# Old-state products as half tiles, and one scaled-query plane for both heads, in the first 16 units of a gated linear attention

## The chip, the cores and the metric

The kernel runs on one core of one Trainium2 chip. The metric is the device time of one execution in microseconds (us). Engines are named as the profile names them: PE (TensorE), DVE (VectorE), ACT (ScalarE), POOL (GpSimd), SP (SyncE, which here issues the DMAs).

## What is computed

A gated linear attention with 4 batches, 8 heads, 768 steps and head size 48, whose output goes through two gated layers:

```python
for t in range(S):
    state = alpha[:, :, t, :, None] * state + einsum('bhd,bhe->bhde', k[:, :, t], v[:, :, t])
    y[:, :, t] = einsum('bhd,bhde->bhe', q[:, :, t], state)
x = y.transpose(0, 2, 1, 3).reshape(B * S, H * D)
h = x @ w_in;  x = (h * cos(h)) @ w_out            # d_ff 2048
a = x @ w_a;   b = x @ w_b;  out = (a * b) @ w_out2 # d_ff 1536
```

## The kernel before

**Units.** The attention is cut into 48 units, one for each batch and each chunk of 64 steps; a unit has all 8 heads, as 4 pairs (p = 2b + c). Within a pair, head 0 lies on rows 64 to 111 and head 1 on rows 0 to 47 (`HEADS`). A unit's steps are, with the lines that the profile shows:

- DVE scans the running product of alpha (L303, tile `ar_t`), takes a reciprocal (L312), scans the other way (L315) and scales the keys (L340, tile `k`; from unit 8 on that last one is POOL's);
- POOL scales the queries into the tile `m` (L327), one operation for each head's 48 rows;
- PE makes scores (L374) and transposed keys (L383), 8 products each;
- ACT copies the keys (L389, tile `kn`), and then DVE masks the scores into `m` (L407; L413 from unit 16 on);
- PE adds up the new state (L444, and L450 for the old state) and makes the outputs: L461 is masked scores times values, and L466 the scaled queries times the old state `s`;
- ACT writes the outputs rounded to `x_t` (L505); DVE then writes the next old state `s` (L535) and the rounding rest of the outputs (L508);
- ACT sums squares for a range test (L344).

A product in f32 is two passes on PE, so 8 products are 16 passes. A unit with an old state in this form, units 1 to 11 and 13 to 15, has 8 products of L466, 224 passes in all. In units 0 to 15 (`APART`) the old state has a tile of its own; later units add it in with the values, on other code that has no L466.

**Rows of the output.** In L461, head 0 of each pair writes rows 0 to 63 of PSUM and head 1 rows 64 to 111. L466 reads 112 rows: for one head the other head's rows of `m` are zero, which is why `m` has three planes (masked scores, and scaled queries of each head beside zeros) that are cleared once at the start (L200).

**Stages.** Units 0 to 7 come first, with a small filler matmul on PE after each (L671). Then the first layer runs in six groups of 512 tokens, with 16 steps each: a projection (L656, tile `hp`), a chain of ACT and DVE operations on it (L706, L709, L714, L717, L721, L725), and the second matmul (L663). Units 8 to 15 stand between the 16 steps of the first group, units 16 to 23 between those of the second, and so on. A step of the first group also needs its weights made from 64-bit words: a DMA (L595, tile `st_t`), ACT (L599, L604), DVE (L610, L616), ACT (L625), POOL (L636). Sixteen such pairs of weights are made until the first group ends. The second layer follows.

**Order.** A planner (`Plan`) sets the order of every engine's instructions before anything runs: each operation has an engine, an assumed length in us, predecessors, and for some a due time; a list schedule over these puts the operations in a row for each engine. Operations marked `port` (two inputs in SBUF on DVE, and POOL's) are kept from overlapping in the planned time. On the chip each engine takes its row in order, so that an instruction that waits holds up all behind it.

**Lines that the change touches.** The tile `m` and its clearing (L198 to L200), the columns of a unit's input load (L284), POOL's scaled queries (L325 to L333), the scores' operand (L376), `outputs` (L455 to L471), and the assumed length of a later unit's block on PE (L494).

Of the kernel before, what the change touches and what calls it, by code (L numbers as in the profile page):

```python
# [10 lines left out]
F32 = mybir.dt.float32  # L11
# [13 lines left out]
C = 64  # L25
# [3 lines left out]
P = 128  # L29
# [28 lines left out]
NLATE = NPAIR2 - NPAIR1  # L58
DVE_DECAY = 0
# [107 lines left out]
def chunked(ctx: ExitStack, tc: tile.TileContext, u_in: bass.AP, wts: bass.AP, out: bass.AP, in_range: bass.AP):  # L167
# [30 lines left out]
    m_t = [att.tile([P, 3, NP, C], F32, name=f"m{i}", bufs=1) for i in range(3)]  # L198
    for i, t in enumerate(m_t):
        (nc.gpsimd if i else nc.vector).memset(t[:, 1:3], 0.0)  # L200
# [55 lines left out]
    def part(u, i):  # L256
        return un[u]["in"][0:112, NA + i * NC4:NA + (i + 1) * NC4].rearrange("p (c t) -> p c t", t=C)
# [16 lines left out]
    def plan_load(u):  # L274
# [3 lines left out]
        def load():  # L278
            if u < UG:
                t = wpool.tile([P, 2, 2 * DM], F32R, name="w_t").bitcast(F32)  # L280
                d["in"] = t.rearrange("p a c -> p (a c)")[:, 0:IN_COLS]
            else:
                d["in"] = att.tile([P, IN_COLS], F32, name="in_t", bufs=NIN)
            cols = W_A + 2 * NE4 if u < APART else IN_COLS  # L284
            cuts = (0, NA + 1, cols) if u == 0 else (0, cols)
            for c0, c1 in zip(cuts, cuts[1:]):
                nc.sync.dma_start(out=d["in"][:, c0:c1], in_=u_in[u, :, c0:c1])
# [5 lines left out]
    def plan_front(u):  # L293
# [20 lines left out]
        def scan_r():  # L314
# [13 lines left out]
                    m[rows, i + apart], part(u, 0)[rows], d["a"][rows, :, 1:], op=ALU.mult  # L328
# [3 lines left out]
            for rows, i in HEADS  # L332
# [29 lines left out]
    def plan_scores(u, block=None):  # L362
# [7 lines left out]
        def score():  # L370
            for c in range(2):
                for b in range(2):
                    for rows, h in HEADS:
                        nc.tensor.matmul(  # L374
                            sc_t[rows_of(b, h), b, c, :], kt[rows, 2 * b + c, :],
                            m[rows, h + apart, 2 * b + c, :], start=True, stop=True,  # L376
# [45 lines left out]
    def plan_back(u):  # L422
# [32 lines left out]
        def outputs():  # L455
            for p in range(NP):
                b, c = divmod(p, 2)
                for h, r0, n in ((0, 0, C), (1, 64, D)):
# [3 lines left out]
                        ys_t[r0:r0 + n, b, c, :], w[0:k_rows], m[0:k_rows, 0 if apart else h, p, :],  # L462
                        start=True, stop=not carry,
                    )
                    if carry:
                        nc.tensor.matmul(  # L466
                            ys_t[r0:r0 + D, b, c, :], s_t[u % 2][:, p * D:p * D + D], m[0:112, h + 1, p, :],
                            start=False, stop=True,
                        )
# [12 lines left out]
        else:  # L482
# [11 lines left out]
            us = ou = op(PE, 1.75 + (1.0 if carry else 0.0), block, [kn, ld, *mk, *ma, *before], due=due)  # L494
# [440 lines left out]
def step_by_step(  # L935
# [76 lines left out]
    with tc.For_i(0, NG, 1) as g:  # L1012
        cols = bass.ds(g * G, G)
        x = pool.tile([P, KT, G], F32, name="g_x", bufs=1)
        for j in range(KT):
            for r0, f0, n in (
                (0, 2 * j * D, D), (48, 6 * D + j, 16), (64, (2 * j + 1) * D, D), (112, 7 * D + j, 16)
# [118 lines left out]
```

## Time and profile before

| | us |
|---|---|
| median of 3 runs | 976.39 (975.45 to 978.84) |
| the profiled execution | 973.26 |
| its span in the trace | 971.4 |
| PE busy | 939.9 (97%) |
| DVE busy | 540.5 (56%) |
| ACT busy | 403.2 (42%) |
| POOL busy | 226.5 (23%) |

Busy times are unions of an engine's instructions over the whole span. They average over stages of different kinds: the first units, the first group with weights being made, the groups with units between the steps, and the second layer.

### The profile page before, as it was taken

The numbers are of one execution on the slowest core, as the hardware profiler recorded it, in microseconds if no ns is written. First come the engines' busy times: TensorE is split into PE (matmuls) and PEld (weight loads), VectorE is DVE, ScalarE is ACT, GpSimd is POOL, SyncE is SP. The second block draws the span as 40 slices with busy tenths as digits, with TensorE's granted clock in tenths as the row PEclk, the third lists the DMA queues.
The fourth block names the chain that finished last, engine by engine and source line by source line (L and its number), as shares of the span: only waits on it lengthen the run. The fifth ranks groups of instructions, "written<-read, shape, count | busy, mean of one in ns | idle before, by whom it ended". The sixth has DMA issues, their size and how long they took to land.

```text
span 971.4 us, 16849 instructions
## 1 busy us (share of the span) xinstructions
PE 939.9 (97%) x6935; PEld 766.3 (79%) x6935; DVE 540.5 (56%) x951; ACT 403.2 (42%) x754; POOL 226.5 (23%) x259
## 2 busy tenths in 40 slices
PE   6798989999999999999999999999999999999996
PEld 4677768888888888888887888888888888888884
DVE  7899998767777786776777842222222222222221
ACT  3477755545545455446665523112113113112111
POOL 4556543313322232312224321001001001000000
PEclk8999999999999999999999999999999999999998
DMA  9355412212221221203223400000000000000000
GB/s 369 106 199 184 164 38 78 90 62 81 88 63 54 89 89 54 64 1 139 98 98 112 149 0 33 1 1 33 1 0 33 1 1 33 0 1 33 1 1 36
DMA packets 17700, 64.96 MB, mean 67 GB/s; under 512 B 2384, under 2 KB 4816, under 8 KB 17616
## 3 DMA queue, kind: packets, MB, share of 16 engines
q1 hardware_dynamic: 17616, 63.81, 19.0%
q8 instruction: 56, 0.92, 0.4%
q14 instruction: 28, 0.23, 0.1%
HBM read 56.72 MB, written 4.72 MB: 63 GB/s over the span
## 4 chain that ended last, share of the span: by engine, by line
PE 87%; DVE 6%; DMA 2%; ACT 2%; issue 1%; POOL 1%; SPq 0%; ACTq 0%
PE acc_t L663 33%; PE hp L656 18%; PE xy L656 15%; PE ap L656 15%; PE xy L461 2%; DMA st_t<-wts 2%; PE xy L374 1%; DVE wf_t L610 1%; DVE wf_t L616 1%; DMA w_t<-u_in 1%; PE xy L383 1%; DVE c_t L709 1%; DVE ar_t L303 1%; PE xy L444 1%; DVE glo_t L725 1%
## 5 line engine op out<-in xcount | busy, mean ns | idle before, releaser
L663 PE MATMUL acc_t<-ghi_t,w_t 128*128 128x512 f32 x972 | 301.1, 391 | 1.0 <-ACT ghi_t L721 1.0
L656 PE MATMUL hp<-x_t,w_t 128*128 128x512 f32 (+1 forms) x882 | 216.4, 390 | 3.2 <-DMA x_t<-x_t 3.2
L663 PEld LDWEIGHTS acc_t<-ghi_t,w_t 128*128 128x128 f32 x972 | 181.6, 188 | 39.3 <-ACT ghi_t L721 1.9
L663 PE MATMUL acc_t<-glo_t,w_t 128*128 128x512 f32 x486 | 190.1, 391 | 3.8 <-DVE glo_t L725 3.8
L822 DVE TENSOR_TENSOR xy<-c_t,xy 128x512 f32<-128x512 f32 x72 | 50.1, 696 | 258.0 <-PE xy L656 257.9
L656 PEld LDWEIGHTS hp<-x_t,w_t 128*128 128x128 f32 x882 | 161.1, 188 | 36.8 <-ACT w_t L625 3.3
L656 PE MATMUL xy<-x_t,w_t 128*128 128x512 f32 x594 | 145.6, 390 | 0.0
L656 PE MATMUL ap<-x_t,w_t 128*128 128x512 f32 x540 | 132.2, 389 | 0.0
L656 PEld LDWEIGHTS xy<-x_t,w_t 128*128 128x128 f32 x594 | 111.5, 188 | 23.4
L656 PEld LDWEIGHTS ap<-x_t,w_t 128*128 128x128 f32 x540 | 101.4, 188 | 21.1
L819 ACT COPY c_t<-ap 128x512 f32<-128x512 f32 x72 | 42.3, 587 | 167.9 <-PE ap L656 167.8
L663 PEld LDWEIGHTS acc_t<-glo_t,w_t 128*128 128x128 f32 x486 | 91.2, 188 | 25.6 <-DVE glo_t L725 6.4
L826 ACT CAST ghi_t<-xy 128x512 fp32r<-128x512 f32 x72 | 42.2, 586 | 138.3 <-DVE xy L822 138.3
L706 ACT ACTIVATE c_t<-hp 128x512 int32<-128x512 f32 x96 | 57.5, 599 | 67.4 <-PE hp L656 67.1
L636 POOL TENSOR_TENSOR w_t<-wf_t,w_t 128x768 fp32r<-128x768 f32 x32 | 64.0, 1999 | 92.1 <-ACT w_t L625 92.1
L781 POOL TENSOR_TENSOR x_t<-x,x_t 128x512 fp32r<-128x512 f32 x18 | 23.7, 1343 | 251.0 <-ACT x_t L778 251.0
L714 ACT ACTIVATE c_t<-c_t 128x512 f32<-128x512 f32 x96 | 60.6, 631 | 46.7 <-DVE c_t L709 45.9
L709 DVE CUSTOM_DVE_ANT_0 c_t<-c_t,hp 128x512 f32<-128x512 int32 x96 | 65.6, 683 | 25.6 <-ACT c_t L706 24.7
L721 ACT CAST ghi_t<-hp 128x512 fp32r<-128x512 f32 x96 | 56.4, 587 | 54.1 <-DVE hp L717 53.5
L717 DVE TENSOR_TENSOR hp<-c_t,hp 128x512 f32<-128x512 f32 x96 | 65.8, 685 | 19.7 <-ACT c_t L714 19.2
L830 DVE TENSOR_TENSOR glo_t<-xy,ghi_t 128x512 fp32r<-128x512 f32 x72 | 49.8, 692 | 47.3 <-ACT ghi_t L826 47.3
L725 DVE TENSOR_TENSOR glo_t<-hp,ghi_t 128x512 fp32r<-128x512 f32 x96 | 65.7, 684 | 17.1 <-ACT ghi_t L721 16.3
(100 smaller groups left out, 923.3 us busy)
## 6 DMA issues: line engine op xcount, KB each, us to landing
st_t<-wts SPq DMA_DIRECT2D x34, 768.0 KB, 4.3
in_t<-u_in SPq DMA_DIRECT2D x32, 626.0 KB, 3.8
in_t<-u_in SPq DMA_DIRECT2D x8, 578.0 KB, 9.5
out<-o_t SPq DMA_DIRECT2D x18, 256.0 KB, 2.1
w_t<-u_in SPq DMA_DIRECT2D x7, 578.0 KB, 7.8
x_t<-x_t SPq DMA_DIRECT2D x48, 48.0 KB, 2.9
w_t<-u_in SPq DMA_DIRECT2D x1, 447.5 KB, 3.5
w_t<-u_in SPq DMA_DIRECT2D x1, 130.5 KB, 2.2
```

The costliest lines, as they stand in the source:

```text
L636: nc.gpsimd.tensor_tensor(t[:, 1], conv.pop(i), t[:, 0].bitcast(F32), op=ALU.subtract)
L656: nc.tensor.matmul(acc, wt[:, w, j * P:(j + 1) * P], r[:, j, :], start=i == 0, stop=i == len(terms) - 1)
L663: nc.tensor.matmul(accs[j], wt[:, w, j * P:(j + 1) * P], r, start=first and i == 0, stop=last and i == 2)
L706: nc.scalar.activation(s["c"].bitcast(I32), s["u"], AF.Identity, bias=-0.25, scale=-1.0)
L709: nc.vector._custom_dve(TENSOR_ADD_SAT, out=s["c"], in0=s["c"].bitcast(I32), in1=s["u"], s0=0.25, s1=-0.75)
L714: nc.scalar.activation(s["c"], s["c"], AF.Sin, bias=math.pi / 2, scale=TWO_PI)
L717: nc.vector.tensor_tensor(s["u"], s["c"], s["u"], op=ALU.mult)
L721: nc.scalar.copy(s["hi"], s["u"])
L725: nc.vector.tensor_tensor(s["lo"], s["u"], s["hi"].bitcast(F32), op=ALU.subtract)
L819: nc.scalar.copy(s["c"], s["a"])
L822: nc.vector.tensor_tensor(s["b"], s["c"], s["b"], op=ALU.mult)
L830: nc.vector.tensor_tensor(s["lo"], s["b"], s["hi"].bitcast(F32), op=ALU.subtract)
```

## The change

In units 0 to 15 the scaled queries of both heads go into one plane of `m` by one POOL operation over 112 rows, in place of two operations over 48 rows into two planes; the tile has two planes, and it is no longer cleared at the start. A product with the old state then reads only its own head's 48 rows, of `s` and of `m`, and stands after the 8 products of L461 in place of between them, in the order that L374 has: c, b, head. The heads write the rows of the output that `rows_of(b, h)` names, so that in pairs 2 and 3 head 0 is on rows 64 to 111; the host's order of the first weights and the fallback follow that. A load of units 0 to 15 has 16 more columns. The planner is told that a later unit's block takes 1.5 us on PE in place of 1.75, plus 0.85 in place of 1.0 where there is an old state.

```diff
-    m_t = [att.tile([P, 3, NP, C], F32, name=f"m{i}", bufs=1) for i in range(3)]
-    for i, t in enumerate(m_t):
-        (nc.gpsimd if i else nc.vector).memset(t[:, 1:3], 0.0)
+    m_t = [att.tile([P, 2, NP, C], F32, name=f"m{i}", bufs=1) for i in range(3)]
...
-            cols = W_A + 2 * NE4 if u < APART else IN_COLS
+            cols = W_A + 2 * NE4 + C - D if u < APART else IN_COLS
...
-                    m[rows, i + apart], part(u, 0)[rows], d["a"][rows, :, 1:], op=ALU.mult
+                    m[rows, i], part(u, 0)[rows], d["a"][rows, :, 1:], op=ALU.mult
...
-            for rows, i in HEADS
+            for rows, i in (((slice(0, 112), 1),) if apart else HEADS)
...
-                            m[rows, h + apart, 2 * b + c, :], start=True, stop=True,
+                            m[rows, 1 if apart else h, 2 * b + c, :], start=True, stop=True,
...
-                for h, r0, n in ((0, 0, C), (1, 64, D)):
+                for h in range(2):
+                    rows = rows_of(b, h)
+                    n = D if rows.start else C
                     w = d["in"][:, W_A + h * NE4 + p * D:W_A + h * NE4 + p * D + n]
                     k_rows = P if apart or h else 112
                     nc.tensor.matmul(
-                        ys_t[r0:r0 + n, b, c, :], w[0:k_rows], m[0:k_rows, 0 if apart else h, p, :],
-                        start=True, stop=not carry,
+                        ys_t[rows.start:rows.start + n, b, c, :], w[0:k_rows], m[0:k_rows, 0 if apart else h, p, :],
+                        start=not carry or c == 0, stop=not carry,
                     )
-                    if carry:
-                        nc.tensor.matmul(
-                            ys_t[r0:r0 + D, b, c, :], s_t[u % 2][:, p * D:p * D + D], m[0:112, h + 1, p, :],
-                            start=False, stop=True,
-                        )
+            if carry:
+                for c in range(2):
+                    for b in range(2):
+                        for rows, h in HEADS:
+                            p, r0 = 2 * b + c, rows_of(b, h).start
+                            nc.tensor.matmul(
+                                ys_t[r0:r0 + D, b, c, :], s_t[u % 2][rows, p * D:p * D + D], m[rows, 1, p, :],
+                                start=False, stop=c == 1,
+                            )
...
-            us = ou = op(PE, 1.75 + (1.0 if carry else 0.0), block, [kn, ld, *mk, *ma, *before], due=due)
+            us = ou = op(PE, 1.5 + (0.85 if carry else 0.0), block, [kn, ld, *mk, *ma, *before], due=due)
```

With other lengths and one POOL operation fewer, the planner puts the instructions of all engines in another order. Line numbers shift too: up to one less before the outputs, five more after them.

ACT near the start, before: `kn0` and `kn1` are the copied keys of even and odd units, `x_t` the outputs (of unit 0, on `xy`, then of unit 1, on `acc_t`), and `wf_t` the first pair of weights.

```order
L505 ACTIVATE x_t_210<-xy_119 112x4x64
L344 ACTIVATE w_t_142,ranges_113<-ar_t_156 112x520
L389 COPY kn1_110<-acc_t_120 128x4x48
L344 ACTIVATE w_t_144,ranges_113<-ar_t_182 112x520
L599 ACTIVATE wf_t_279<-st_t_216 128x768
L505 ACTIVATE x_t_210<-acc_t_120 112x4x64
L389 COPY kn0_109<-xy_119 128x4x48
```

The same place now, from the square sum of unit 2 on:

```order
L343 ACTIVATE w_t_141,ranges_110<-ar_t_199 112x520
L510 ACTIVATE x_t_220<-acc_t_117 112x4x64
L388 COPY kn0_106<-xy_116 128x4x48
L604 ACTIVATE wf_t_317<-st_t_255 128x768
L343 ACTIVATE w_t_147,ranges_110<-ar_t_260 112x520
L388 COPY kn1_107<-acc_t_117 128x4x48
L510 ACTIVATE x_t_220<-xy_116 112x4x64
```

The first weights' conversion stood ahead of the outputs of unit 1; now it stands behind them and behind the keys of unit 2, and ahead of the keys of unit 3 and the outputs of unit 2.

DVE near the start, before, from the reciprocal of unit 1 on (scans are printed as SCALAR_TENSOR_TENSOR with `first` or `last`): `m0` and `m1` are the masked scores of units 0 and 1, `k1` and `k0` the keys of units 1 and 2, `s1` the old state for unit 1.

```order
L312 RECIPROCAL last_91<-ar_t_156 112x4
L315 SCALAR_TENSOR_TENSOR ar_t_156<-w_t_142,last_91 112x260
L340 TENSOR_TENSOR k1_108<-ar_t_156,w_t_142 112x256
L303 SCALAR_TENSOR_TENSOR ar_t_182<-w_t_144,first_90 112x260
L407 TENSOR_TENSOR m0_99<-xy_119,mask_95 128x256
L312 RECIPROCAL last_91<-ar_t_182 112x4
L315 SCALAR_TENSOR_TENSOR ar_t_182<-w_t_144,last_91 112x260
L340 TENSOR_TENSOR k0_107<-ar_t_182,w_t_144 112x256
L303 SCALAR_TENSOR_TENSOR ar_t_212<-w_t_150,first_90 112x260
L535 TENSOR_TENSOR s1_106<-xy_119,ar_t_146 112x192
L508 SCALAR_TENSOR_TENSOR x_t_210<-xy_119,x_t_210 112x4x64
```

The same place now:

```order
L311 RECIPROCAL last_91<-ar_t_153 112x4
L314 SCALAR_TENSOR_TENSOR ar_t_153<-w_t_139,last_91 112x260
L406 TENSOR_TENSOR m0_99<-xy_116,mask_95 128x256
L339 TENSOR_TENSOR k1_105<-ar_t_153,w_t_139 112x256
L302 SCALAR_TENSOR_TENSOR ar_t_199<-w_t_141,first_90 112x260
L311 RECIPROCAL last_91<-ar_t_199 112x4
L540 TENSOR_TENSOR s1_103<-xy_116,ar_t_143 112x192
L406 TENSOR_TENSOR m1_100<-acc_t_117,mask_95 128x256
L314 SCALAR_TENSOR_TENSOR ar_t_199<-w_t_141,last_91 112x260
L339 TENSOR_TENSOR k0_104<-ar_t_199,w_t_141 112x256
L513 SCALAR_TENSOR_TENSOR x_t_220<-xy_116,x_t_220 112x4x64
```

The mask of unit 0 moved ahead of the keys of unit 1 and of the first scan of unit 2, and the next state and the mask of unit 1 ahead of the second scan of unit 2; scans of units further on moved behind.

DVE at the fourth pair of weights, before (`wf_t` with two numbers is that pair and the next; `ar_t` with `first` is the scan of a unit further on):

```order
L709 ISA c_t_796<-c_t_796,hp_756 128x512
L616 SCALAR_TENSOR_TENSOR wf_t_754<-st_t_545,wf_t_754 128x768
L717 TENSOR_TENSOR hp_756<-c_t_796,hp_756 128x512
L303 SCALAR_TENSOR_TENSOR ar_t_855<-in_t_389,first_90 112x260
L610 SCALAR_TENSOR_TENSOR wf_t_848<-wf_t_848,st_t_680 128x768
L535 TENSOR_TENSOR s0_105<-xy_119,ar_t_643 112x192
L312 RECIPROCAL last_91<-ar_t_855 112x4
L725 TENSOR_TENSOR glo_t_877<-hp_756,ghi_t_872 128x512
```

The same place now:

```order
L714 ISA c_t_779<-c_t_779,hp_741 128x512
L621 SCALAR_TENSOR_TENSOR wf_t_739<-st_t_610,wf_t_739 128x768
L722 TENSOR_TENSOR hp_741<-c_t_779,hp_741 128x512
L615 SCALAR_TENSOR_TENSOR wf_t_766<-wf_t_766,st_t_655 128x768
L302 SCALAR_TENSOR_TENSOR ar_t_855<-in_t_410,first_90 112x260
L730 TENSOR_TENSOR glo_t_860<-hp_741,ghi_t_853 128x512
L540 TENSOR_TENSOR s0_102<-xy_116,ar_t_638 112x192
L714 ISA c_t_845<-c_t_845,hp_789 128x512
```

The first conversion of the next pair stood behind the scan; now it stands ahead of it.

## Rows read from the trace of the kernel before

**Rows 1.** A row for each stretch; the first line names the columns
```profile
core 0: us, PE busy (x) PEld busy (x) DVE busy (x) ACT busy (x) POOL busy (x), PEclk, DMA share, GB/s
0.00:41.00 41.00, 30.91 (x684) 23.20 (x684) 30.14 (x67) 17.90 (x41) 19.12 (x33) 0.92 0.67 257
41.00:134.00 93.00, 81.27 (x914) 65.06 (x914) 87.93 (x128) 65.86 (x119) 56.34 (x42) 0.98 0.48 162
134.00:437.00 303.00, 303.00 (x3034) 245.55 (x3034) 229.73 (x493) 153.09 (x319) 91.24 (x149) 1.00 0.20 65
```

**Rows 2.** Timeline of ACT, then DVE: start us, us, instruction, [idle before <- releaser]
```profile
18.62 0.90 ACT L599 ACTIVATE wf_t<-st_t 128x768 f32<-128x768 f32 x1 [5.53 <-DMA st_t<-wts]
19.43 0.36 ACT L505 ACTIVATE x_t<-acc_t 112x256 fp32r<-112x256 f32 x1
19.70 0.30 ACT L389 COPY kn<-xy 128x192 f32<-128x192 f32 x1
...
20.69 0.63 ACT L344 ACTIVATE w_t<-ar_t 112x520 f32<-112x520 f32 x1
21.21 0.20 ACT L344 ACTIVATION_READ_ACCUMULATOR w_t<-ar_t 112x1 f32 x1
...
19.41 0.43 DVE L340 TENSOR_TENSOR k<-ar_t,w_t 112x256 f32<-112x256 f32 x1 [3.16 <-PE xy L383]
...
20.10 0.41 DVE L407 TENSOR_TENSOR m<-xy,mask 128x256 f32<-128x256 f32 x1
```

**Rows 3.** The chain that ended last, first units: start us, us, what
```profile
32.46 0.56 PE acc_t L450 x4
33.03 0.26 PE acc_t L461 x3
...
34.13 0.19 PE acc_t L671
...
41.21 0.39 ACT x_t L505
```

**Rows 4.** Timeline around the first projection step, DVE and PE
```profile
41.63 0.43 DVE L508 SCALAR_TENSOR_TENSOR x_t<-acc_t,x_t 112x256 fp32r<-112x256 f32 x1 [0.41 <-ACT x_t L505]
41.97 0.35 DVE L535 TENSOR_TENSOR s<-acc_t,ar_t 112x192 f32<-112x192 f32 x1
...
43.05 0.93 DVE L616 SCALAR_TENSOR_TENSOR wf_t<-st_t,wf_t 128x768 int32<-128x768 int32 x1
...
45.72 1.44 PE L656 MATMUL hp<-x_t,w_t 128*128 128x256 f32 x9 [3.22 <-DMA x_t<-x_t]
```

**Rows 5.** The chain that ended last, unit 9 on PE
```profile
57.02 0.33 PE xy L461 x4
57.34 0.12 PE xy L466 x4
...
58.16 0.39 PE xy L374 x16
58.55 0.22 PE xy L383 x16
```

**Rows 6.** Groups by line from 41 to 134 us: xcount, busy us, mean ns
```profile
L610 DVE SCALAR_TENSOR_TENSOR wf_t<-wf_t,st_t 128x768 int32<-128x768 int32 x15 | 20.9, 1396 | 0.1
L616 DVE SCALAR_TENSOR_TENSOR wf_t<-st_t,wf_t 128x768 int32<-128x768 int32 x15 | 17.2, 1150 | 0.0
L303 DVE TENSOR_TENSOR_SCAN ar_t<-in_t,first 112x260 f32<-112x260 f32 x8 | 11.0, 1380 | 0.0
...
L636 POOL TENSOR_TENSOR w_t<-wf_t,w_t 128x768 fp32r<-128x768 f32 x15 | 29.7, 1981 | 24.1 <-ACT w_t L625 24.1
L327 POOL TENSOR_TENSOR m<-in_t,ar_t 48x256 f32<-48x256 f32 x18 | 17.6, 977 | 4.7 <-DVE ar_t L303 4.0
```

**Rows 7.** One line, whole execution: xcount, ns min/median/max, first and last start
```profile
L610 DVE SCALAR_TENSOR_TENSOR wf_t<-wf_t,st_t x34: 923/954/3280, 32.2 to 562.1; 128x768 int32<-128x768 int32 x34
...
L303 DVE TENSOR_TENSOR_SCAN ar_t<-in_t,first x40: 666/700/2998, 35.4 to 409.6; 112x260 f32<-112x260 f32 x40
```

More of the change, by code (lines that the diff above doesn't have):

```diff
@@ L58 @@
 NLATE = NPAIR2 - NPAIR1
+LOW, HIGH = (0, 2, 5, 7), (1, 3, 4, 6)
 DVE_DECAY = 0
@@ L1016, in step_by_step @@
             for r0, f0, n in (
-                (0, 2 * j * D, D), (48, 6 * D + j, 16), (64, (2 * j + 1) * D, D), (112, 7 * D + j, 16)
+                (0, LOW[j] * D, D), (48, LOW[3] * D + j, 16), (64, HIGH[j] * D, D), (112, HIGH[3] * D + j, 16)
             ):
@@ L1107 @@
     perm = np.stack([
-        np.concatenate([rows[2 * j], rows[6, j::KT], rows[2 * j + 1], rows[7, j::KT]])
+        np.concatenate([rows[LOW[j]], rows[LOW[3], j::KT], rows[HIGH[j]], rows[HIGH[3], j::KT]])
         for j in range(KT)
```

## The prediction

> **What bounds the kernel now.** I first cut the execution into stretches [rows 1]. From 134 us on PE is busy without a gap (303.00 of 303.00 us): from there the end is PE's remaining work, and nothing that ACT, DVE or POOL gain there counts. From 41 to 134 us, where the weights of the first group are made, DVE is busy 87.93 of 93 us, PE 81.27 and POOL 56.34. In the first 41 us no engine is full: PE 30.9, DVE 30.1, POOL 19.1. So the first 134 us are what can shrink, and a saving on PE alone is worth little in them.
>
> Next I read what the first units wait for. ACT takes its row in order, and from 13.1 to 18.62 us it stands 5.53 us before the first weights' conversion L599, until its DMA lands [rows 2]. Behind that stood the outputs of unit 1 (L505, at 19.43, 0.81 us after the conversion began). DVE waited 3.16 us meanwhile. From there on the units follow one another: the outputs of unit 7 are read at 41.21 [rows 3], so six units took 21.78 us, 3.63 each. Then the first projection's second half waits on PE for the DMA of the outputs of units 4 to 7, until 45.72 [rows 4], 3.66 us after DVE finished them (41.63 + 0.43).
>
> In the stretch from 41 to 134 us DVE's own rows are longer than they need be. L610 takes 1396 ns there on average and L303 1380 ns [rows 6], where their medians are 954 and 700 ns, and single ones take up to 3280 and 2998 ns [rows 7]. Over the counts that is 15 x 0.44 = 6.6 us, 8 x 0.68 = 5.4 us, and for L616, which has L610's shape, 15 x 0.20 = 2.9 us: 14.9 us in all. These operations read two inputs in SBUF, as POOL's do; L717 and its like, which read PSUM, are not among the long ones. I take the long ones for waits for a POOL operation that has begun, mostly the weights' L636 of 1.98 us [rows 6]. I call one a lock.
>
> **The order at the start: -3.4 us.** This is the largest term, and it comes from the planner's new order, not from the work removed. ACT's row now has the outputs of unit 1 and the keys of unit 2 ahead of the first conversion. I assume that the DMA lands when it did; each input load grows by 16 columns on 1156, 1.4%, which I cost at nothing (at most 1.4% of the 18.62 us until then, 0.3 us). When the wait ends at 18.62, one unit more is done. Then ACT has the conversion (0.8 us until the next one starts), a square sum with its read-out (20.69 to 21.41, 0.72 us) and the keys of unit 3 (0.30 us) [rows 2]: keys of unit 3 ready at 20.5.
>
> From keys to keys a unit now goes through: mask 0.41 [rows 2], new keys' product on half tiles 0.22 [rows 5], old state 0.56 [rows 3], L461 0.26 [rows 3] and three further groups of 0.12 [rows 5], together 0.62, the half tiles of the old-state products 0.39 (below), the filler matmul 0.19 [rows 3], scores and transposes 0.39 + 0.22 [rows 5], keys' copy 0.30: 3.30 us. For four changes of engine I add 0.2 (one is 0.03: 41.60 to 41.63 [rows 3, 4]): 3.5 us. Keys of unit 7 come at 20.5 + 4 x 3.5 = 34.5, and its outputs are read 0.41 + 0.22 + 0.56 + 0.62 + 0.39 = 2.2 us and a change or two later, at 36.9 in place of 41.21: 4.3 us sooner. At the old pace of 3.63 it would be 3.8.
>
> How much of this survives? On PE, the second half of the first projection: outputs done at 36.9 + 0.39 + 0.43 = 37.7, plus the DMA's 3.66, gives 41.4 in place of 45.72: -4.3. On DVE, the end of the second pair's L616: from 37.3, what its new row has up to there, 0.43 + 0.35 [rows 4], two scans of 0.70 and an L610 and an L616 of 0.95 [rows 7], ends at 41.4 in place of 43.98 [rows 4]: -2.6. The next stage hangs on DVE more than on PE, and on both; I take the middle, -3.4, with -2.6 and -4.3 as ends.
>
> **POOL's one operation for two: -0.5 us.** Sixteen of 32 operations go. In units 8 to 15 that is 8 of the 18 L327 of the stretch, at 0.98 us [rows 6], 7.8 of POOL's 56.34 us. POOL isn't full there, and waits 24.1 us for ACT before L636 alone. If locks fell with POOL's time, it would be 14.9 x 7.8 / 56.34 = 2.1 us; if all are L636's, nothing. I take 0.5, nearer to nothing, since a single L303 of 3.0 us holds more than an L327. For units 0 to 7 the saving is within the pace above, in which POOL's row doesn't come last.
>
> **The old-state products on PE: 0.** In unit 9 they are half of 32 passes from 57.02 to 58.16, 1.14 us, in groups of four of 0.12 us, so two passes run side by side [rows 5]. Scores and transposes are half tiles of the shape that L466 gets: 16 passes in 0.39 us behind products of full rows, and in 0.22 without such a change [rows 5], so four run side by side and the change of shape costs 0.17. For units 8 to 11 and 13 to 15, where scores follow, it is now 0.33 + 3 x 0.12 + 0.39 + 0.22 = 1.30 us to the end of the scores in place of 1.53 (57.02 to 58.55): 7 x 0.23 = 1.6 us less. PE idles 11.7 us in that stretch [rows 1], so I credit nothing; the end is 1.6 if PE is what waits last. In units 1 to 7 the sum is 1.01 in place of 1.10 (33.03 to 34.13 [rows 3]), which is in the pace, and the filler behind it changes shape once more, beside ACT.
>
> Here a page speaks against the change. In L374 and L383 the two heads of a pair stand on different row halves and write one PSUM bank, and the 16 passes still take 0.22 us, a quarter of what they would take one by one. The Trainium skill, TensorEngine Tiling (Array Packing), section Restrictions and Gotchas, says under Gotcha 1 that different row tiles can't access the same PSUM bank at one time; by that they would go in pairs at best, 0.46 us, and the row disagrees.
>
> **Edits at nothing.** The cleared planes (three operations) ran before the first input was there. From unit 16 on, head 1 follows head 1 on the same rows once in each output block. The halves go in pairs now, and I expect each half to keep its own row; if not, a pass of 0.06 us [rows 5] is added in each of 32 blocks, in a stretch that PE bounds: +1.8 at most. The planner's 1.5 for 1.75 us moves steps of later groups by a place; PE has no gap there for it to cost or win.
>
> **The sum.** -3.4 - 0.5 = -3.9 us. The profiled execution took 973.26 us (span 971.4), 3.1 below the median of the runs, and would take 969.4; on the median's footing 976.39 - 3.9 = 972.5.
>
> **The rivals.**
> Slower: more locks. The new order puts L610 ahead of the scan at the fourth pair of weights, right where POOL's L636 of the third or fourth starts, and other places change likewise. Each lock costs DVE up to 1.98 us. There are now 14.9 us of them, worth about eight. Two more undo the gain, three and a half make it a loss beyond 0.3%; four more give -3.9 + 7.9 = +4.0, 980.4 us. For it: fifteen L636 meet some forty two-input operations, with nothing on the chip that keeps them apart. Against it: the patterns behind each L616 look alike in both orders.
>
> Little change: the lead is spent. The first conversion on DVE stands behind the units' work as before, so the first pair and the projections come no sooner, and DVE in the next stage is 95% busy. If a third of DVE's smaller lead lasts, -2.6 / 3 = -0.9: 975.5.
>
> Much faster: three locks fewer, -5.9, with the lead of 3.4: -9.3, 967.1. PE's idle 11.7 us would allow it.
>
> The half tiles don't run four abreast: 0.46 for 0.22 in the five units from 3 to 7, +1.2, so -2.7: 973.7. The page above has this; the rows of L374 speak against it.
>
> **How the numbers follow.** A measurement of this kernel can tell about 0.3% (2.9 us) from no change, so faster means under 973.5. The forecast has 0.46; its own ends are -4.3 - 2.1 - 1.6 = -8.0 and -2.6 + 1.8 = -0.8, and four fifths of it lie under 973.5. More locks 0.12, the lead spent 0.26, fewer locks 0.13, paired half tiles 0.03. Faster: 0.37 + 0.13 + 0.02 = 0.52; same: 0.09 + 0.26 + 0.01 = 0.36; slower: 0.12. The range goes from 967.0, with fewer locks just inside, to 978.5, where half of the slower case is out.
>
> **What would show it.** In the changed kernel ACT's wait for the first weights should end near 18.6 us with the outputs of unit 1 already done, the outputs of unit 7 be read near 37 us, and the first projection's second half start near 41.5. L466's passes should come in groups of four of some 0.06 us. L610, L616 and L303 should have the same 14 to 15 us above their medians, less half a microsecond. PE should run without a gap from about 130 us on. It is wrong if the conversion's DMA lands later, if L610 and L303 in that stretch lengthen, or if PE waits as long as before for the first group's weights.

## The result: slower, and the clock of the first units is why

| | median of the runs, us | profiled execution, us | span, us | mean granted clock |
|---|---|---|---|---|
| before | 975.92 (975.3 to 978.84) | 973.26 | 971.4 | 0.991 |
| after | 986.18 (984.71 to 989.16) | 985.47 | 983.7 | 0.966 |

The ratio is 1.0103 with a 95% interval of 1.0071 to 1.0135: the changed kernel is slower by some 10 us, where 972.5 was forecast, and outside the range of 967.0 to 978.5. Here and below, a median is of all executions of a kernel but those over 1,050 us (four in all, two of them of the kernel before). A ratio is to the executions of before that were taken beside it, and leaves out those that lie over 1.5% above the fastest of their kernel, among them some with a low clock.

The page of after shows where to look before any wait is read. Its forty slices of the span give PE's busy share and the clock that it was granted, in tenths:

```profile
PE   7779989999999999999999999999999999999996
...
PEclk7559999999999999999999999999999999999998
```

The second and third slice, some 25 to 74 us, stand at half. The same in ten-microsecond stretches of after (busy time of each engine, then PEclk, DMA share, GB/s):

```profile
core 0: us, PE busy (x) PEld busy (x) DVE busy (x) ACT busy (x) POOL busy (x), PEclk, DMA share, GB/s
10.00:20.00 10.00, 8.16 (x158) 6.41 (x154) 4.95 (x13) 3.88 (x11) 1.36 (x2) 0.57 1.02 417
20.00:30.00 10.00, 7.70 (x144) 5.68 (x140) 4.72 (x12) 3.94 (x9) 1.36 (x2) 0.50 0.60 238
30.00:40.00 10.00, 8.29 (x138) 6.60 (x138) 5.19 (x13) 3.42 (x8) 1.37 (x2) 0.50 0.08 22
40.00:50.00 10.00, 7.52 (x139) 5.67 (x136) 4.74 (x10) 2.18 (x7) 0.00 (x0) 0.50 0.01 2
50.00:60.00 10.00, 7.71 (x67) 6.36 (x70) 7.00 (x12) 3.94 (x6) 5.40 (x5) 0.50 0.37 113
60.00:70.00 10.00, 7.19 (x130) 6.82 (x123) 6.14 (x11) 6.04 (x13) 4.81 (x4) 0.53 0.56 205
70.00:80.00 10.00, 10.00 (x121) 8.11 (x120) 8.20 (x15) 7.09 (x14) 3.87 (x4) 1.00 0.43 140
```

TensorE runs at 1.2 GHz (granted 0.50) from 11.5 to 69.5 us, 58 us long. In the kernel before it did so from 12.6 to 19.4 and from 46.7 to 50.1, 10.2 us together. Two stretches of the kernel before:

```profile
20.00:30.00 10.00, 7.75 (x221) 6.49 (x223) 7.76 (x20) 7.12 (x16) 2.71 (x4) 1.00 0.59 234
30.00:40.00 10.00, 8.99 (x247) 7.44 (x243) 7.68 (x17) 5.04 (x11) 4.92 (x6) 1.00 0.31 102
```

A busy PE hides this: 7.5 busy microseconds of ten look like a PE that works as it did, but at half the clock. DVE, whose mask takes 0.42 us here and took 0.41 before [rows 2], shows it: from 20 to 40 us it is busy 4.72 and 5.19 of ten, for 7.76 and 7.68.

Against [rows 1], the first three stretches of after:

```profile
0.00:41.00 41.00, 31.69 (x521) 22.71 (x525) 20.88 (x51) 14.64 (x33) 7.40 (x19) 0.64 0.62 240
41.00:134.00 93.00, 83.90 (x1054) 68.20 (x1047) 75.99 (x125) 65.17 (x119) 49.71 (x33) 0.85 0.48 165
134.00:437.00 303.00, 300.33 (x2958) 242.76 (x2957) 232.41 (x493) 153.28 (x320) 95.70 (x151) 0.99 0.21 67
```

PE is as busy in the first 41 us (31.69 for 30.91), and does 521 matmuls in them where it did 684. This is one unit of after on PE (start us, us, instruction, idle time before it and who ended it):

```profile
17.79 0.68 PE L443 MATMUL xy<-w_t,kn 64*48 64x48 f32 x16 [0.94 <-DVE m L406]
18.39 1.06 PE L449 MATMUL xy<-s,ident 112*112 112x96 f32 x4
19.38 1.12 PE L462 MATMUL xy<-m,w_t 128*64 128x64 f32 x16
20.43 0.68 PE L471 MATMUL xy<-m,s 48*48 48x64 f32 x16
21.04 0.63 PE L676 MATMUL acc_t<-zeros 128*64 128x512 bf16 x1
22.28 0.70 PE L373 MATMUL acc_t<-m,k 48*64 48x64 f32 x16 [0.61 <-DVE x_t L513]
```

PE works 4 to 5 us and then waits 0.94 us for the mask; that wait stands ahead of every unit's new keys. A unit takes some 6 us here. The 0.61 us before L373 come from the filler: the operation of DVE that L373 waits for waited in its turn for L676, which writes a bank of the tile that it reads,

```profile
21.71 0.42 DVE L513 SCALAR_TENSOR_TENSOR x_t<-acc_t,x_t 112x256 fp32r<-112x256 f32 x1 [2.92 <-PE acc_t L676]
```

and this comes back in every second unit (at 22.28, 34.67 and 47.07).

What ACT and PE say of the forecast's own places (rows of after that answer to [rows 2, 3, 4]):

```profile
15.84 0.38 ACT L510 ACTIVATE x_t<-acc_t 112x256 fp32r<-112x256 f32 x1 [2.10 <-PE acc_t L676]
...
18.09 0.90 ACT L604 ACTIVATE wf_t<-st_t 128x768 f32<-128x768 f32 x1 [0.82 <-DMA st_t<-wts]
...
53.03 0.38 ACT L510 ACTIVATE x_t<-acc_t 112x256 fp32r<-112x256 f32 x1 [2.25 <-PE acc_t L676]
...
57.50 2.26 PE L661 MATMUL hp<-x_t,w_t 128*128 128x256 f32 x9 [2.29 <-DMA x_t<-x_t]
```

ACT's long wait went as forecast: 0.82 us for 5.53 [rows 2], with the outputs of unit 1 read before it. But the outputs of unit 7 are read at 53.03, against 41.21 [rows 3], and the projection's second half begins at 57.50, against 45.72 [rows 4]: 11.8 us later at both places. The span ends 12.3 us later.

### The profile page after: what moved, and what is told of

Read it like the earlier page. It is cut to its first block, busy times and chain, and to the rows that moved or that the text cites. A ratio compares the mean times of both kernels' runs of the same rounds, so it can differ in the third digit from the quotient of the medians.

```text
span 983.7 us, 16811 instructions
## 1 busy us (share of the span) xinstructions
PE 953.4 (97%) x6935; PEld 776.4 (79%) x6935; DVE 530.1 (54%) x950; ACT 404.9 (41%) x754; POOL 213.6 (22%) x241
## 3 DMA queue, kind: packets, MB, share of 16 engines
HBM read 56.85 MB, written 4.72 MB: 63 GB/s over the span
## 4 chain that ended last, share of the span: by engine, by line
PE 91%; DVE 4%; DMA 2%; ACT 1%; issue 1%; SPq 0%; ACTq 0%; DVEq 0%
PE acc_t L668 33%; PE hp L661 19%; PE xy L661 15%; PE ap L661 15%; PE xy L462 3%; DMA st_t<-wts 2%; PE xy L373 2%; PE xy L443 1%; PE xy L382 1%; DVE wf_t L621 1%; PE xy L449 1%; DMA w_t<-u_in 1%; DVE wf_t L615 0%; PE acc_t L676 0%; PE acc_t L462 0%
## 5 line engine op out<-in xcount | busy, mean ns | idle before, releaser
L661 PE MATMUL hp<-x_t,w_t 128*128 128x512 f32 (+1 forms) x882 | 219.4, 395 | 2.3 <-DMA x_t<-x_t 2.3
L661 PEld LDWEIGHTS hp<-x_t,w_t 128*128 128x128 f32 x882 | 164.0, 193 | 36.9 <-issue 3.0
L827 DVE TENSOR_TENSOR xy<-c_t,xy 128x512 f32<-128x512 f32 x72 | 50.1, 696 | 258.0 <-PE xy L661 257.9
L722 DVE TENSOR_TENSOR hp<-c_t,hp 128x512 f32<-128x512 f32 x96 | 65.7, 684 | 20.1 <-ACT c_t L719 20.1
L726 ACT CAST ghi_t<-hp 128x512 fp32r<-128x512 f32 x96 | 56.4, 587 | 48.2 <-DVE hp L722 47.7
```

The lines of the kernel that those rows point to most:

```text
L661: nc.tensor.matmul(acc, wt[:, w, j * P:(j + 1) * P], r[:, j, :], start=i == 0, stop=i == len(terms) - 1)
L722: nc.vector.tensor_tensor(s["u"], s["c"], s["u"], op=ALU.mult)
L726: nc.scalar.copy(s["hi"], s["u"])
L827: nc.vector.tensor_tensor(s["b"], s["c"], s["b"], op=ALU.mult)
```

## The experiments

Each execution comes with its mean granted clock. That turned out to be what tells one execution of a kernel from another, so I count an execution as **clock up** from 0.984 on; the profiled one of before, with 10.2 us at 1.2 GHz in its first 70, has 0.991, that of after 0.966. The border is mine, set after the clocks were known, and no gap in the numbers marks it: those of before run from 0.979 to 0.992. Where the executions of a kernel lie far apart, the median and the count of clock up say more than the ratio.

| kernel | median, us | ratio to before [95%] | clock up |
|---|---|---|---|
| before | 975.8 | | 90 of 120 |
| after | 986.2 | 1.0103 [1.0071, 1.0135] | 0 of 4 |
| half tiles, old order | 979.2 | 1.0026 [1.0014, 1.0038] | 0 of 10 |
| old instructions, new order | 980.8 | 1.0034 [1.0007, 1.0061] | 4 of 10 |
| after, products over 112 rows | 985.0 | 1.0098 [1.0079, 1.0116] | 0 of 6 |
| after, two POOL operations | 989.0 | 1.0138 [1.0109, 1.0167] | 0 of 6 |
| after, 2 fillers a unit | 981.9 | 1.0057 [1.0035, 1.0078] | 0 of 10 |
| after, 3 more in the gap | 979.0 | 1.0040 [1.0013, 1.0067] | 7 of 12 |
| before, 3 more in the gap | 979.6 | 1.0053 [1.0036, 1.0070] | 5 of 5 |
| half tiles, old order, 3 more | 982.2 | 1.0058 [1.0027, 1.0089] | 5 of 12 |
| after, filler in a free bank | 982.2 | 1.0087 [1.0053, 1.0121] | 1 of 6 |
| after, free bank, 2 more | 971.7 | 0.9978 [0.9957, 0.9999] | 11 of 12 |
| after, free bank, 4 more | 972.8 | 0.9965 [0.9944, 0.9986] | 11 of 11 |
| before, free bank, 4 more | 978.2 | 1.0023 [1.0005, 1.0042] | 12 of 12 |
| half tiles, old order, free bank, 4 more | 974.2 | 0.9982 [0.9968, 0.9996] | 12 of 12 |
| after, free bank, 4 more in units 0 to 2 | 978.3 | 0.9996 [0.9971, 1.0021] | 3 of 12 |
| after, free bank, 4 more from unit 3 | 972.9 | 0.9987 [0.9965, 1.0009] | 9 of 12 |
| before without filler | 976.4 | 1.0002 [0.9981, 1.0022] | 6 of 12 |

### One part of the change at a time

**Half tiles in the old order.** The changed instructions in the order of the kernel before, held there by an empty second POOL step in the plan and the old lengths:

```diff
+            ma = [
+                op(POOL, 0.7, lambda: scale_q(slice(0, 112), 1), [sa, *m_before], port=True),
+                op(POOL, 0.7, lambda: None, [sa, *m_before], port=True),
+            ]
-            us = ou = op(PE, 1.5 + (0.85 if carry else 0.0), block, [kn, ld, *mk, *ma, *before], due=due)
+            us = ou = op(PE, 1.75 + (1.0 if carry else 0.0), block, [kn, ld, *mk, *ma, *before], due=due)
```

> The changed kernel's instructions (half tiles, one POOL operation for the scaled queries) in the order of the kernel before: the planner is given the old lengths and an empty second POOL operation. Theory FORM (half tiles keep PE at the half clock through the first units, whatever the order): the clock falls near 12 us and stays at 1.2 GHz until about 70 us, time 984 to 988 us. Theory ORDER (the new order spaces PE's work so that the clock doesn't rise again): the clock is back by about 20 us as before, time 973 to 977 us.

979.2 us; in the profiled execution 1.2 GHz from 11.2 to 48.8.

**The old instructions in the new order.** Both POOL operations in one planned step, and the new lengths:

```diff
+        def both():
+            for rows, i in HEADS:
+                scale_q(rows, i)
+            ma = [op(POOL, 0.7, both, [sa, *m_before], port=True)]
-            us = ou = op(PE, 1.75 + (1.0 if carry else 0.0), block, [kn, ld, *mk, *ma, *before], due=due)
+            us = ou = op(PE, 1.5 + (0.85 if carry else 0.0), block, [kn, ld, *mk, *ma, *before], due=due)
```

> The kernel before's instructions (old-state products on 112 rows, two POOL operations, cleared planes) in the order of the changed kernel. Theory FORM: the clock rises again by about 20 us, and the lead of the new order, 3 to 4 us, shows: 970 to 974 us. Theory ORDER: the clock stays at 1.2 GHz until about 70 us as in the changed kernel, 985 to 989 us.

980.8 us, but the executions range from 973.0 at a clock of 0.990 to 988.8 at 0.969: one program, 16 us apart, and the clock goes with it. So neither theory stands alone: each half of the change costs 3 to 5 us and both together 10.

**Products over 112 rows.** If half tiles were what kept the clock down, full rows in the changed kernel would bring it back:

```diff
-    ys_t[r0:r0 + D, b, c, :], s_t[u % 2][rows, p * D:p * D + D], m[rows, 1, p, :],
+    ys_t[r0:r0 + D, b, c, :], s_t[u % 2][0:112, p * D:p * D + D], m[0:112, 1, p, :],
```

> The changed kernel with each old-state product over 112 rows of both operands instead of one head's 48, so that no two of them run side by side by rows; its place in the order, POOL's one operation and everything else stay. Its sums take in the other head, so the outputs differ; the work it times is that of full tiles. Theory FORM (PE's shorter burst per unit with half tiles is what keeps the clock down): the clock rises before 30 us and the time is 976 to 981, as for the old instructions in the new order (980.8). Rival ORDER (the spacing alone keeps it down): 1.2 GHz to past 45 us, 984 to 987.

985.0: in the new order the rows of the tiles are not what costs the time. The clock of the profiled execution did rise before 30 us, as FORM had it, but only from 22.2 to 25.6; it was at 1.2 GHz again until 46.1. The run also bounds what half tiles cost or gain as such where the clock is down: 986.2 against 985.0, with intervals that overlap. In the old order half tiles were not taken apart from POOL's one operation.

**Two POOL operations into the one plane**, rows 64 to 111 and 0 to 63:

```diff
+        def both():
+            for rows in (slice(64, 112), slice(0, 64)):
+                scale_q(rows, 1)
```

> The changed kernel with its scaled queries made by two operations on POOL, one head's rows each, into the same plane; order and half tiles as changed. Theory GAP (POOL's operation ends before PE asks for it either way, so the gap for the mask stays 0.93 us): within 1.5 us of the changed kernel, 984 to 988. Rival POOL (the single operation shifts the units' spacing so that the clock stays down): 979 to 982, as for the old instructions in the new order.

989.0, with 2.8 us more than after and intervals that still overlap: POOL's one operation doesn't cause the loss, and may be worth a gain. What else sets the old instructions in the new order (980.8) apart from these two, such as the alternation of L461 and L466, was not tried.

### Filler

**More filler behind the outputs, and none.** Two matmuls of zeros in place of one behind each unit of after; and the kernel before with none there (`keep_warm(0)`).

```diff
-                keep_warm(1)
+                keep_warm(2)
```

> The changed kernel with two filler matmuls in place of one after each of the first eight units, nothing else. If the half clock is what costs the time, and more PE work holds it up, the clock is back at 2.4 GHz by about 20 us and the time is 970 to 975 us, 11 to 16 us below the changed kernel; FORM and ORDER both allow it. If the time comes from something else (POOL and DVE in each other's way, weights that come late), it stays within 1 us of 986, or gets worse by 8 fillers of 0.2 to 0.6 us, 2 to 5 us.

981.9, 4 us less than after; 1.2 GHz from 22.2 to 53.0 us and from 56.4 to 66.6 in the profiled execution, in place of 11.5 to 69.5. The rise by 20 us and the 970 to 975 us didn't come: this filler is too little, or stands in the wrong place.

> The kernel before without the filler matmul after each of the first eight units. If the clock in the first units hangs on how much PE has to do, it should stay at 1.2 GHz here too, until 60 to 70 us, and the time be 983 to 990 us with the old form and the old order. If the old form or the old order alone is enough to bring the clock back, it is at 2.4 GHz from about 20 us and the time is 974 to 977 us.

A single execution took 973.3 us, at a clock of 0.989; twelve more show no gain:

> The kernel before without the filler behind the outputs of units 0 to 7 (15 at the start stay), which took 973.3 in one run. If that holds, its filler costs 2 us and the clock needs no filler in the old form: 972.5 to 974.5. Rival (chance in the single run): 975 to 977.

976.4, with 6 of 12 executions clock up, where 90 of 120 are with the filler. That is too few to show that the filler is worth something to the clock in the old form; on the time the two agree.

**Three more where PE waits for the mask**, behind the transposes of units 0 to 8, in three kernels:

```diff
+            def front():
+                for fn in ops["emit"]:
+                    fn()
+                keep_warm(3)
```

> The changed kernel with three further filler matmuls behind the transposes of units 0 to 8, where PE waits 0.90 to 0.94 us for the mask; no other instruction moves. Theory CLOCK (all that was lost is lost because PE stays at 1.2 GHz through the first units; the change's own work would gain what was forecast): the granted clock is at 2.4 GHz from about 25 us at the latest, the three fillers (0.64 us at 2.4 GHz) lie inside the wait, and the time is 971 to 974. Rival LATER (the order of DVE and POOL in the weights' stretch loses as well): the clock rises as early, the time stays at 977 or more. Rival SPACING (filler cannot hold the clock up in this order): 1.2 GHz until past 45 us again, 980 or more.

> The kernel before with the same three fillers behind the transposes of units 0 to 8: the control for the run above. Theory CLOCK: the kernel before has only 10 us at 1.2 GHz in its first 70 us, so filler can give it at most half of that on PE and nothing where ACT's wait sets the pace: 975 to 976.5. Rival (filler is worth several us in any form, so that the run above says nothing on the change): 972 or less.

> Half tiles and POOL's one operation in the order of the kernel before, with the same three fillers: clock held up, the old order. It prices the new order with the clock equal. Forecast's first term (the new order is worth 3.4 us where the clock is up): 975 to 976, 3 to 4 us above the changed kernel with the same fillers. Rival (the lead is spent in the weights' stretch): within 1 us of it. Rival LATER: 2 us or more below it.

The executions of after fall in two: seven at 976.0 to 979.3 with a clock of 0.986 and more, five at 989.3 to 995.3 with 0.973 and less. So the clock went as CLOCK had it in seven and as SPACING had it in five, and CLOCK's time, 971 to 974, came in none: filler cost the kernel before 3.8 us, too. The trace of after with three fillers, an execution with a low clock, shows one way in which it costs (ACT's read of a unit's outputs):

```profile
16.13 0.38 ACT L515 ACTIVATE x_t<-acc_t 112x256 fp32r<-112x256 f32 x1 [1.91 <-PE acc_t L681]
```

L681 is the filler. It writes the accumulator's first bank and the odd units stand in the other two of the same tile, so ACT waits for filler that was issued behind the outputs. (It is not the only way: four fillers in a bank of their own, below, still cost the kernel before 2.3 us.) Where the clock was up, half tiles in the old order took 976.3 and in the new order 978.0, before 979.6: the first sign that half tiles and POOL gain and that the order doesn't.

**The filler in a bank that no unit uses**, four in the gap:

```diff
-        warm = acc_t[:, 0]
+        warm = bank("hp", "hp", 3)
...
+                keep_warm(4)
```

> The changed kernel with four filler matmuls behind the transposes of units 0 to 8, and with all filler written to a bank that no unit uses, so that no reader of a unit's bank waits for a filler (in the run with three fillers ACT's read of the outputs waited 1.91 us for them). Theory CLOCK: the clock stays at 2.4 GHz from 20 us on at the latest and the time is 971 to 975; with the clock equal, the runs with three fillers put the new order 1.6 us above the old one and half tiles with POOL's one operation some 3 us below full tiles, so 973 to 974 here. Forecast's first term (the order gains 3.4 us where the clock is up): 970 to 972, and 3 us below the same kernel in the old order. Rival SPACING (filler in the gaps does not hold the clock up): 1.2 GHz past 45 us in most runs, 980 or more.

> The kernel before with the same four fillers in the free bank. Theory CLOCK with filler off the path: 974 to 976, as the kernel before, since its clock is up anyway. Rival (the fillers themselves cost, as the three in a unit's bank did: 980.4): 979 or more.

> Half tiles and POOL's one operation in the old order, with the same four fillers in the free bank. Theory CLOCK, from the runs with three fillers (976.3 where the clock was up, against 979.5 for full tiles): 971 to 973, the fastest of the three. Forecast's first term: 975 to 976, 3 us above the new order. Rival (half tiles keep the clock down whatever fills the gaps): 980 or more with 1.2 GHz past 40 us.

The clock is up in all 35 executions counted. The changed kernel takes 972.8, 3.0 us less than the kernel before; with the same filler it is 5.3 us below the old form. Its first units, the same stretches and columns as above:

```profile
10.00:20.00 10.00, 9.94 (x229) 6.50 (x225) 6.29 (x16) 4.26 (x13) 2.05 (x3) 1.00 1.02 418
20.00:30.00 10.00, 9.16 (x208) 6.30 (x210) 7.86 (x20) 6.35 (x15) 1.37 (x2) 1.00 0.70 269
```

229 matmuls, the fillers among them, in the ten microseconds from 10 on, for 158 of after.

**The bank alone, and two fillers.**

> The changed kernel with its filler written to a bank that no unit uses, no filler added. Theory GAP (the clock stays down since PE has a gap of 0.93 us in every unit): 1.2 GHz to past 45 us as in the changed kernel, 984 to 987. Rival BANK (what the four-filler run gained came from readers that no longer wait for a filler): 973 to 977.

> The changed kernel with two fillers in the gap in place of four, in the free bank. Theory GAP: two fill 0.43 of the 0.93 us at 2.4 GHz and 0.86 at 1.2 GHz; the clock is up in most runs but falls in some, 973 to 979, with a wider spread than with four (973.0). Rival BANK: as with the bank alone, within 1 us.

The bank alone leaves 982.2 in the middle, and gives what I could not have ordered: its profiled execution kept the clock (0.988) and took 972.48, the other five 980.6 to 988.7 at 0.964 to 0.974. Order and work are those of after; only the place that filler is written to differs. That place may have a part in the time as well: the five at a low clock have a median of 983.6, 2.6 us under after, with ranges that overlap. The clock of the one execution stays up until 43.3, and is at 1.2 GHz from there to 57.0:

```profile
10.00:20.00 10.00, 6.96 (x213) 5.29 (x208) 6.16 (x17) 4.20 (x13) 2.05 (x3) 1.00 1.02 419
```

though PE waits for the mask in every unit as before, 0.94 us; this is one unit of it on PE:

```profile
15.86 0.45 PE L443 MATMUL xy<-w_t,kn 64*48 64x48 f32 x16 [0.94 <-DVE m L406]
16.24 0.63 PE L449 MATMUL xy<-s,ident 112*112 112x96 f32 x4
16.80 0.68 PE L462 MATMUL xy<-m,w_t 128*64 128x64 f32 x16
17.41 0.44 PE L471 MATMUL xy<-m,s 48*48 48x64 f32 x16
17.78 0.40 PE L676 MATMUL hp<-zeros 128*64 128x512 bf16 x1
18.12 0.46 PE L373 MATMUL acc_t<-m,k 48*64 48x64 f32 x16
```

Beside the unit of after above, these rows are the cost of the clock: L449 0.63 for 1.06, L462 0.68 for 1.12, L471 0.44 for 0.68. With two fillers the clock is up in 11 of 12 executions and the median is 971.7, the lowest of all.

**Early gaps or late ones.** The four fillers in the gaps of units 0 to 2 alone, and (with `u >= 3`) in those of units 3 to 8 alone:

```diff
-                keep_warm(4)
+                keep_warm(4 if u < 3 else 0)
```

> The changed kernel, filler in the free bank, four more behind the transposes of units 0 to 2 alone. Theory START (a clock that is up at the third unit stays up, gaps of 0.94 us or not, as in the one fast run with the bank alone): 971 to 974 in nearly all runs. Rival GAPS (the gaps of the later units pull it down again): falls to 1.2 GHz between 20 and 35 us in most runs, 976 to 984.

> The same, with the four fillers behind the transposes of units 3 to 8 alone. Theory START: the clock falls near 11.5 us in most runs as in the changed kernel, and comes back only when units 3 and 4 leave PE no gap at 1.2 GHz (1.7 us of filler in 0.93): up from 30 us at the latest, 974 to 977. Rival GAPS: what the later gaps pull down doesn't come, 971 to 974, as with filler in all units.

Filler in units 0 to 2 alone leaves the clock up in 3 of 12 (978.3; 1.2 GHz from 20.1 to 64.5 in the profiled one), filler from unit 3 on in 9 of 12 (972.9). START fell: with the first three gaps filled the clock stayed up in only 3 of 12. The gaps of the later units count, and filling them suffices in most executions.

## Why the prediction was wrong, point by point

**The step that failed: every duration of PE was taken at 2.4 GHz.** The term "order at the start" sums a unit to 3.5 us from rows of the kernel before whose matmuls ran at the full clock, and carries that clock over to an order in which it didn't hold. The PEclk of 0.92 stands in [rows 1], and the working never asks what kept it there. At 1.2 GHz a unit takes 6 us, seven of them come 11.8 us late, and the rest of the kernel, which PE bounds, starts that much later.

The execution with the bank alone, against after, shows what the clock did (ACT and PE, columns as above):

```profile
38.02 0.38 ACT L510 ACTIVATE x_t<-acc_t 112x256 fp32r<-112x256 f32 x1 [0.38 <-PE acc_t L471]
...
42.48 1.59 PE L661 MATMUL hp<-x_t,w_t 128*128 128x256 f32 x9 [1.91 <-DMA x_t<-x_t]
```

Outputs of unit 7 at 38.02 for 53.03, the second half at 42.48 for 57.50, both 15.0 us apart; the spans are 970.8 and 983.7, 12.9 apart. Not all of the 15.0 is the clock's. With filler in the free bank and 1.2 GHz from 20.1 us on (the profiled execution with early gaps filled) the outputs of odd units are read 11.73 us apart, 5.87 a unit:

```profile
23.79 0.38 ACT L515 ACTIVATE x_t<-acc_t 112x256 fp32r<-112x256 f32 x1 [0.45 <-PE acc_t L476]
...
47.26 0.38 ACT L515 ACTIVATE x_t<-acc_t 112x256 fp32r<-112x256 f32 x1 [1.72 <-PE acc_t L476]
```

In after they are 6.20 a unit (28.23 to 53.03); the 0.61 us of every second unit make nearly all of the difference. Three such waits, by 0.61 us each, make 1.8 us for the bank, an estimate that leaves some 13 for the clock. That the working let the filler's bank cost nothing is a second step that failed, a smaller one.

This execution took 972.48 us, and that it lies next to the 972.5 of the forecast is luck. The working gives 969.4 for a profiled execution, from the 973.26 of before; 0.8 us was gained here, not 3.9, and 12.2 lost in the kernel as it is.

**The sum with the clock held up came nearer, by other terms.** With the clock up in all executions (four fillers in the free bank), the new order is worth 972.82 - 974.21 = -1.4 us, not -3.4, and the intervals of the two overlap; half tiles with POOL's one operation 974.21 - 978.15 = -3.9, not -0.5, and those intervals do not overlap. One term was 2.0 us too large and the other 3.4 too small; that their sum, -5.3, isn't farther from -3.9 is luck again. The four fillers cost the old form 2.3 us, so a part of the 3.9 may be room for filler that shorter products leave; how much is open.

- *The pace.* 3.5 us was forecast for a unit; the keys of units 3 to 7 are copied at 19.65 to 35.13 in the execution with the bank alone, 3.87 each. The working took the filler at 0.19 and the new keys at 0.22, where from start to start they take 0.34 (17.78 to 18.12) and 0.38 (15.86 to 16.24). Hence 38.02 for 36.9.
- *What survives.* In that execution the second half came on PE 3.24 us sooner than in the kernel before (42.48 for 45.72), against -4.3; the end of the second pair's L621 on DVE 0.6 sooner (43.34 for 43.98), against -2.6. The span is 0.6 us shorter, as DVE's end has it, and near the -0.9 of the rival in which the lead is spent. Its reason holds, too: the first L615 starts at 33.35, no sooner than L610 at 32.2 [rows 7].

```profile
42.17 1.17 DVE L621 SCALAR_TENSOR_TENSOR wf_t<-st_t,wf_t 128x768 int32<-128x768 int32 x1
```

- *ACT's wait and the load.* As forecast: the conversion starts at 18.09 in after and at 18.23 with the bank alone, for 18.62, so the longer loads cost nothing that shows.
- *The old-state products.* Half tiles went as the row of L374 had it, and not in pairs: 16 passes from 17.41 to 17.78, 0.37 us, where 0.39 was forecast. They start in groups of four, the last three at 17.50, 17.56 and 17.62.
- *Locks.* They fell, as the rival with fewer of them had it, and gave little for it. The groups by line from 41 to 134 us of after (count, busy us, mean ns), against [rows 6]:

```profile
L621 DVE SCALAR_TENSOR_TENSOR wf_t<-st_t,wf_t 128x768 int32<-128x768 int32 x15 | 17.6, 1171 | 0.0
L615 DVE SCALAR_TENSOR_TENSOR wf_t<-wf_t,st_t 128x768 int32<-128x768 int32 x15 | 14.6, 972 | 0.0
...
L302 DVE TENSOR_TENSOR_SCAN ar_t<-in_t,first 112x260 f32<-112x260 f32 x9 | 6.7, 744 | 0.0
```

  L615 has 972 ns for L610's 1396, L302 744 for 1380. Over medians of 952 and 699 that is 0.3 + 0.4 us, with L621's 3.3 some 4 us in place of 14.9. With the clock up (bank alone) the same groups are:

```profile
L621 DVE SCALAR_TENSOR_TENSOR wf_t<-st_t,wf_t 128x768 int32<-128x768 int32 x15 | 18.6, 1243 | 0.0
L615 DVE SCALAR_TENSOR_TENSOR wf_t<-wf_t,st_t 128x768 int32<-128x768 int32 x14 | 13.7, 976 | 0.0
...
L302 DVE TENSOR_TENSOR_SCAN ar_t<-in_t,first 112x260 f32<-112x260 f32 x10 | 9.2, 923 | 0.0
```

  Now they add up to 6.9 us, so a part of the fall in after may have come with the slow units, but not L615's. That one goes with the order: of the profiled executions in the new order, eight have 970 to 987 ns for this line and three 1115 to 1246; the eight in the old order have 1213 to 1434. The rival put 5.9 us on three locks. Eight us of them went, and PE, idle 10.1 us in the stretch for 11.73, gained 1.6. With the bank alone, the stretches from 41 to 134 and from 134 to 437 us are

```profile
41.00:134.00 93.00, 82.90 (x918) 67.02 (x919) 82.22 (x130) 67.69 (x120) 51.76 (x36) 0.92 0.48 162
134.00:437.00 303.00, 303.00 (x3030) 245.35 (x3030) 227.52 (x488) 152.84 (x319) 92.11 (x150) 1.00 0.20 65
```

- *PE without a gap from 130 us on.* Not in after, 300.33 of 303 us; with the bank alone 303.00.

**The slower rival** had the right sign and the wrong mechanism. None of the cases with a price let the clock move, so the 0.12 on slower rested on locks, which fell.

**Why the clock went down, and what stays open.** In the kernel before, one piece of PE's work stands right ahead of the rise: PE ran without idle time, at 1.2 GHz, from 14.30 (L444) to 19.34 (L383), and the clock rose at 19.4. These are the first and the last row of that piece:

```profile
14.30 0.68 PE L444 MATMUL acc_t<-w_t,kn 64*48 64x48 f32 x16 [2.27 <-DVE m L407]
...
18.72 0.62 PE L383 MATMUL xy<-ident,k 48*64 48x48 f32 x16
```

With half tiles in the old order the same piece is 0.1 us shorter (14.44 to 19.36) and the clock stayed down until 48.8. In the new order every unit has its gap of 0.9 us, and the pieces between are 4.9 us at most (24.31 to 29.23 in after). Their length alone doesn't explain the clock: in the old instructions in the new order a piece of 5.0 us (12.12 to 17.15) was not followed by a rise until 22.1. What is shown: with filler in the gaps, in the free bank, the clock is up (11 of 11, 11 of 12), the later gaps matter more than the first ones, and in the new order the rows of the tiles matter little. In the old order half tiles and POOL's one operation together cost 3.4 us and left the clock up in none of ten; which of the two does it is open. Open is also why the execution with the bank alone kept its clock through gaps of 0.94 us and five others of the same program didn't.

The traces hold one lead that no run tests by itself, PE's idle time ahead of unit 0's new keys. In the nine profiled executions whose clock fell between 9.7 and 12.6 us it was 1.5 to 3.3 us, in the ten others 0.2 to 1.8. It was 2.19 in after and 1.71 in that with the bank alone: the keys come at 9.14 and 9.21, but the filler at the start ended at 6.34 and at 6.89.

The Trainium skill, TensorE: Matmul & The Clock Gate, section Part 1: The HAM clock gate (the "warmup" mystery), says that the number of slow matmuls at a kernel's start varies from run to run, and that for modeling the ramp's penalty is under 1% of a typical kernel's span, so that one shouldn't fit a specific count. That the share of slow work varies from execution to execution agrees with the clocks here. The second part can't be carried over to this kernel, whose clock falls again after the start: two executions of one program, the old instructions in the new order, are 973.0 and 988.8 us, 1.6% apart.

## What to carry to other kernels

Before summing durations for a new order, read the granted clock of the stretch in both, and ask what the engine did there that kept it up: here a shorter chain with a gap in every unit lost more by the clock than it gained by its length. A saving that takes TensorE's work away from a stretch that something else bounds should be tried with filler in the freed gap, written to a bank that nobody waits for, before it is judged. Where executions of one program differ, sort them by their clock before comparing medians; here 972.5 and 983.6 us (the median of the five others) were one program.

## What the chip showed that I had not expected

- TensorE was busy 7.2 to 8.3 us of every ten from 10 to 70 us and was granted 1.2 GHz from 11.5 to 69.5; the four executions of after have mean clocks of 0.964 to 0.969.
- One program (the old instructions in the new order) took 973.0 to 988.8 us, in step with mean clocks of 0.990 to 0.969.
- Two fillers of some 0.2 us in a wait of 0.93 us, with all filler in a bank that no unit uses, took 14.5 us off the changed kernel: 971.7 for 986.2. The bank alone took off 4.0. The 971.7 is also 4.1 us below the kernel before, with an interval (0.9957 to 0.9999) that ends next to no change, so the gain over the kernel before is small if it is one.
